# Hash attention and an MLP mixer on one core: three head pairs sorted by two hash bits where there were two

## The chip, the core and the metric

The kernel runs on one core of a Trainium2 chip. The metric is device time in microseconds (us), the median of three runs of one compiled program; profiles are of one further execution. TensorE is called PE in profile lines (its weight loads PEld), VectorE DVE, ScalarE ACT, GpSimd POOL, and SyncE SP; SP and POOL issue the DMAs.

## The reference

Four batches of eight heads, 768 tokens, head size 64. Each token of q and k gets a bucket from the signs of six projections, and a query attends only to keys of its own bucket. The heads side by side make a 768 x 512 matrix per batch, which goes through a mixer over tokens and one over channels. The weights come as 64-bit floats.

```python
q_bucket = np.sum((np.einsum('bhsd,dk->bhsk', q, proj) > 0) * powers, axis=-1)   # k_bucket likewise
mask = q_bucket[:, :, :, None] == k_bucket[:, :, None, :]
scores = np.where(mask, scale * np.matmul(q, k.transpose(0, 1, 3, 2)), -1000000000.0)
attn = np.exp(scores - np.max(scores, axis=-1, keepdims=True))
x = np.matmul(attn / (np.sum(attn, axis=-1, keepdims=True) + 1e-09), v)          # heads are then put side by side
u = x + (np.maximum(x.transpose(0, 2, 1) @ w_tok1, 0.0) @ w_tok2).transpose(0, 2, 1)
out = u + np.maximum(u @ w_ch1, 0.0) @ w_ch2
```

## The kernel before

**Stages.** The program has three stages: attention, tokens, channels. Attention works on 16 pairs of heads, numbered 0 to 15; pair n is heads 2(n mod 4) and the next of batch n // 4. `XT` holds the result, channels on partitions, and is the working copy of the activations to the end. A guard that is computed along the way chooses a slower exact path if scores could overflow; it isn't taken with these inputs. The order of instructions within a stage is the order of the code.

**A regular pair** (0 to 13). PE makes scores, `scores` (L487), the 6-bit mask added through a product of bits; ACT takes the exponential into `exps` (L414); DVE adds the exponentials over key blocks into `esd` (`add` and `add_last`, L446 to L459); PE sums `esd` with a product by ones (L536) and weighs v (`weigh`, L470); DVE makes reciprocals (`newton`, L549 and L551, ACT copying rows at L557) and multiplies (`divide`, L561). The loop over pairs (L1012) interleaves this: while pair n is scored, pair n-1 is divided. Hash bits of a pair two ahead are made in between and spread by DMAs of SP (L373) and POOL (L376).

**The conversion of weights.** A 768-column piece of 64-bit weights becomes 32-bit in one ACT instruction (L177) and five DVE instructions (L187, L191, L195, L196, L206). Attention converts twelve pieces, one in each of pairs 0, 1 and 3 to 12: first the token weights `W1` (two pieces) and `W2` (two), then eight of the channel weights `WC1`. Tokens converts eight pieces of the second channel weight.

**A sorted pair** (14 and 15, class `Sorted`). Two of the six bits put every token in one of four groups of 256 slots, so that scores are needed only within a group. Its steps are hung into the loop of the regular pairs by the dictionary `SORTED` and the calls of `at`, in three numbers `(first, made, back)`. In pair `first` the tokens are hashed and counted; in the next three, POOL writes 24 blocks of rows into tables in DRAM (`scatter`, L791, eight in each, alternating with the bit DMAs); in the pair ahead of `made`, SP fetches the sorted rows (L801 to L809) and DVE turns q (`turn_q`, L820); at `newton` of pair `made`, DVE turns k (L820) and the bits (`turn_sorted_bits`, L833). At the end of pair `made`, after the regular weighing, PE makes the sorted scores (L848), sums and weighing (L862, L874), and DVE divides and turns back (L889 to L899) ahead of the next pair's adds. SP writes the result in slot order (L902). POOL then gathers twelve blocks back to token order (`gather`, L908), in pairs `back` and the next, the last four each followed by two small memsets (`pause`, L940), and SP stores them (L918).

**Order between the stages.** Token matrices (tokens on partitions) pass through DRAM, one matrix `bounced` per batch: `bounce` transposes two pairs on DVE (L233) and SP writes them (L238). `fetch` (L245) reads a batch into `x0` (batches 0, 2) or `x1` (1, 3). SP runs its DMAs in order, so what waits at its head holds all behind it. `x0` of batch 0 is fetched at the end of pair 12. In pair 13 two more pairs are bounced (`bounce_late`), right after `newton`; then comes the fetch of `x1` for batch 1. Sorted pairs must also reach `XT`: SP reads them back (`fetch_turned`, L929) and DVE transposes them there (`finish`, L935) at the end of attention.

**Tokens** runs, per batch b, `mix1(b)` (24 passes of PE at L1222), then the second product of batch b-1 in two halves (`mix2`, L1262) with five DVE additions each (L1277 to L1281); POOL adds each half to `XT` by a DMA (L1282). `mix2` has three buffers, and its PSUM banks come free as DVE reads them. Channels (L1349 and around) follows, nearly all PE.

## Time and profile before

| | us |
|---|---|
| median of three runs (lowest, highest) | 768.08 (767.57, 768.83) |
| profiled execution, its own time | 766.84 |
| its span on the core | 765.1 |
| attention, to the first product of tokens | 288.05 |
| tokens, to the first product of channels | 78.5 |
| channels | 398.5 |

The profiled execution is 1.24 us below the median of the runs, and 1.7 us of it lie around the span. PE counts as busy for 99% of the span and DVE for 88%, but PE's ends are modelled, so a busy PE says only that it has work queued; the rate is read from how far apart equal pieces start. Rows of the timeline give start, duration, engine, line, operation, what is written and read, how many, and in brackets how long the engine was idle before and what released it.

### The profile page before, as it was taken

The page shows a single profiled execution, that of the slowest core. Times are in us where ns is not written, and L with a number is a line of the kernel's source. Part 1 is how long each engine was busy: PE and PEld are TensorE (multiplying, and loading weights), DVE is VectorE, ACT ScalarE, POOL GpSimd, SP SyncE. Part 2 cuts the span into 40 slices and gives each one's busy share as a digit, 9 for nine tenths or more (in the row PEclk, how much of TensorE's full clock was granted, in tenths as well). Part 3 has the DMA queues.
Part 4 walks back from the last instruction along what each step waited for, and adds up shares of the span by engine and source line. Part 5 has one row for each costly group of instructions (what it writes and reads, how often), then busy time and mean ns, then how long its engine had stood idle before and what let it go on. Part 6 is the DMA issues. An engine that isn't in the chain of part 4 may idle for free.

```text
span 765.1 us, 14575 instructions
## 1 busy us (share of the span) xinstructions
PE 757.4 (99%) x5549; PEld 507.8 (66%) x5549; DVE 672.7 (88%) x965; ACT 444.8 (58%) x820; POOL 188.5 (25%) x266
## 2 busy tenths in 40 slices
PE   8999999999999999999999999999999999999997
PEld 4555555665656554555444468888878888886886
DVE  5899899999998898999788798998899799889884
ACT  6677777677777773333222326566666667665331
POOL 2346772647761810011220100110000011000001
PEclk9999999999999999999999999999999999999999
DMA  7756578664965549876697997889566696750655
GB/s 257 271 172 178 179 243 231 199 207 142 222 198 117 168 67 263 313 168 123 113 316 253 349 359 259 246 227 280 169 220 212 236 259 141 233 158 10 205 162 126
DMA packets 131210, 157.80 MB, mean 206 GB/s; under 512 B 56000, under 2 KB 99520, under 8 KB 129216
## 3 DMA queue, kind: packets, MB, share of 16 engines
q1 hardware_dynamic: 119248, 136.05, 56.1%
q0 software_dynamic: 11600, 20.53, 13.2%
q8 instruction: 45, 0.74, 0.4%
q10 hardware_dynamic: 288, 0.25, 0.1%
q14 instruction: 29, 0.24, 0.1%
HBM read 107.71 MB, written 40.67 MB: 194 GB/s over the span
## 4 chain that ended last, share of the span: by engine, by line
PE 81%; DVE 12%; ACT 2%; issue 2%; DMA 1%; POOL 1%; DVEq 0%; ACTq 0%; SPq 0%; POOLq 0%
PE b L1349 51%; PE sc L503 12%; PE acc L470 11%; ACT exps L414 1%; PE sc L425 1%; DVE size L196 1%; DVE esd L459 1%; PE ss L848 1%; DVE unit L195 1%; PE hash L536 1%; PE sacc L874 1%; DMA XT<-second 1%; DVE second L206 1%; DVE size L191 1%; DVE unit L187 1%
## 5 line engine op out<-in xcount | busy, mean ns | idle before, releaser
L1349 PE MATMUL b<-R,second 128*128 128x256 f32 (+1 forms) x522 | 131.8, 408 | 0.0
L414 ACT ACTIVATE exps<-sc 128x768 f32<-128x768 f32 (+1 forms) x181 | 126.5, 765 | 8.9 <-PE sc L503 6.1
L503 PE MATMUL sc<-qk 32*128 32x384 f32 (+1 forms) x1352 | 119.3, 458 | 0.0
L1349 PEld LDWEIGHTS b<-R,second 128*128 128x128 f32 x522 | 99.2, 190 | 28.4 <-issue 16.5
L470 PE MATMUL acc<-exps,vn 128*32 128x385 f32 (+1 forms) x1344 | 111.7, 486 | 0.0
L503 PEld LDWEIGHTS sc<-qk 32*128 32x128 f32 x1352 | 91.7, 185 | 17.2 <-issue 4.5
L1355 ACT COPY c<-b 128x256 f32<-128x256 f32 (+1 forms) x96 | 40.3, 427 | 79.4 <-PE b L1349 66.1
L470 PEld LDWEIGHTS acc<-exps,vn 128*32 128x32 f32 x1344 | 43.8, 109 | 62.0 <-issue 59.6
L376 POOL DMA_DIRECT2D bits<-XT x104 | 54.5, 526 | 70.8 <-issue 38.6
L459 DVE TENSOR_TENSOR esd<-esd,exps 128x768 f32<-128x768 f32 x70 | 66.9, 956 | 4.3
L1349 PE MATMUL b<-XT,WC 128*128 128x256 f32 (+1 forms) x208 | 61.0, 428 | 0.0
L791 POOL DMA_INDIRECT table<-XT,sorting x48 | 56.3, 1173 | 15.0 <-issue 13.8
L2059 POOL DMA_DIRECT2D out<-second x7 | 8.5, 1213 | 186.8 <-DVE second L2053 81.7
L1349 PEld LDWEIGHTS b<-XT,WC 128*128 128x128 f32 x208 | 39.5, 190 | 15.4 <-issue 10.3
L503 PE MATMUL sc<-bits 32*128 32x384 bf16 (+1 forms) x338 | 48.0, 311 | 0.1
L557 ACT COPY rec<-rec 32x384 f32<-32x384 f32 x56 | 28.6, 510 | 33.0 <-DVE rec L551 31.5
L1349 PE MATMUL b<-XT,SW 128*128 128x256 f32 (+1 forms) x164 | 47.0, 410 | 0.0
L455 DVE TENSOR_TENSOR esd<-esd,exps 128x768 f32<-128x768 f32 x42 | 40.2, 958 | 4.4
L1222 PE MATMUL t<-x,W 128*128 128x512 f32 x96 | 42.1, 594 | 0.2 <-DMA x<-bounced 0.2
L1349 PEld LDWEIGHTS b<-XT,SW 128*128 128x128 f32 x164 | 31.1, 190 | 9.4 <-issue 4.1
L1282 POOL DMA_DIRECT2D XT<-second x8 | 9.9, 1233 | 97.6 <-DVE unit L187 58.0
L1222 PEld LDWEIGHTS t<-x,W 128*128 128x128 f32 x96 | 18.1, 190 | 23.3 <-issue 21.7
(332 smaller groups left out, 1452.7 us busy)
## 6 DMA issues: line engine op xcount, KB each, us to landing
second<-left SPq DMA_DIRECT2D x20, 768.0 KB
qk<-in_qk_rows SPq DMA_DIRECT2D x13, 1152.0 KB
raw<-in_moe_w_ch SPq DMA_DIRECT2D x16, 768.0 KB
second<-left SPq DMA_DIRECT2D x18, 576.0 KB
WC<-hidden_left SPq DMA_DIRECT2D x18, 448.0 KB
x<-bounced SPq DMA_DIRECT2D x4, 1536.0 KB
XT<-second POOLq DMA_DIRECT2D x8, 768.0 KB
seen<-in_qk SPq DMA_DIRECT2D x15, 384.0 KB
```

The lines of the kernel that those rows point to most:

```text
L376: nc.gpsimd.dma_start(out=to[at : at + 2 * BITS, half[j]], in_=g[of : of + 2 * BITS])
L414: return nc.scalar.activation(e[:, :, columns], sc, ACT.Exp, scale=SCALE)
L455: nc.vector.tensor_tensor(self.d, self.d, e, op=ALU.add)
L459: nc.vector.tensor_tensor(self.d, self.d, e, op=ALU.add)
L470: made = nc.tensor.matmul(acc[D * i + d : D * i + d + 32], vn[:, i, c, d : d + 32], e[:, i], start=(c == 0), stop=(c == NR - 1),)
L503: nc.tensor.matmul(made[j, piece][:, i], k[at : at + 32, ks], q[at : at + 32], start=part < 0, stop=part == 1,)
L557: nc.scalar.copy(rec[other : other + 32, h], rec[at : at + 32, h])
L791: nc.gpsimd.indirect_dma_start(out=tables[2 * w + i], out_offset=bass.IndirectOffsetOnAxis(ap=self.at[:, x : x + 1], axis=0), in_=row, in_ ...
L1222: nc.tensor.matmul(ps, W1[:, r, P * j : P * j + P], x[:, r], start=(r == 0), stop=(r == NR - 1),)
L1282: nc.gpsimd.dma_start(out=XT[:, 2 * m : 2 * m + 2, S * b : S * b + S], in_=to.rearrange("p i n t -> p i (n t)"), accum_op=ALU.add,)
L1349: nc.tensor.matmul(ps, left(k), right(k), start=start and k == ks[0], stop=stop and k == ks[-1], skip_group_check=True,)
L1355: nc.scalar.copy(c, ps)
```

## The change

`SORTED` gets a third entry, so pair 13 is sorted too and the loop has 13 regular pairs (0 to 12). Its third number is now how many scatters go in each of three pairs. The entries are 13: first 1, made 6; 14: first 4, made 9; 15: first 7, made 11. There are two sets of DRAM tables in place of one, the second cleared in pair 2. The channel weights are converted first, then `W1`, then `W2`, whose last piece falls in pair 12, now the last; until then `W1` and `W2` hold q, k and v of the sorted pairs.

For pair 15, `made` isn't `first + 5`, so its sorted rows are fetched at the end of pair 10, and all its turning stands at a new point, `turned`, in pair 11 behind the conversion. All 36 gathers stand behind POOL's last hash DMAs: ten in pair 11, ten in pair 12 and sixteen in tokens, each with a `pause`. The stores of pairs 14 and 15, `fetch_turned` (into `x0`, free after `mix1(2)`) and `finish` move into tokens, `finish` just ahead of the second product of batch 3. The bounce in the last pair comes after the first `divide`.

```diff
-    SORTED = {B * NP - 2: (1, 6, 9), B * NP - 1: (5, 10, 11)}
+    SORTED = {B * NP - 3: (1, 6, (8, 8, 8)), B * NP - 2: (4, 9, (8, 8, 8)), B * NP - 1: (7, 11, (10, 10, 4))}
...
+            for x, count in enumerate(counts):
+                at(first + 1 + x, "indirect", *[call("scatter")] * count)
+            if made == first + 5:
+                at(made - 1, "begin", call("fetch"))
+                at(made - 1, "last", call("turn_q"))
+                at(made, "sums", call("copy_bits"))
+                at(made, "newton", call("turn_k"), call("turn_sorted_bits"))
+            else:
+                at(made - 1, "last", call("fetch"))
+                at(made, "weighed", call("copy_bits"))
+                at(made, "turned", call("turn_q"), call("turn_k"), call("turn_sorted_bits"))
             at(made, "end", call("scores", 0), call("scores", 1), call("weigh"))
             at(made, "last", call("divide"), call("turn_back"))
...
+            gathers += [call("gather", r, i) for r in range(NR) for i in range(2)]
+            stores.append((n, call("store")))
+        for n in (NREG - 2, NREG - 1):
+            for _ in range(10):
+                at(n, "indirect", gathers.pop(0), pause)
+        for gather in gathers:
+            remaining.extend((gather, pause))
...
+        at(2, "loads", lambda: clear_tables(1))
+        at(NREG - 1, "newton", stores.pop(0)[1])
...
-            [(w_tok1, W1, 3, (0, NR)), (w_tok2, W2, 1, (0, NJ)), (w_ch1, WC1, 1, (0, NCB))],
+            [(w_ch1, WC1, 1, (0, NCB)), (w_tok1, W1, 3, (0, NR)), (w_tok2, W2, 1, (0, NJ))],
...
-            converts = n not in (2, NREG - 1)
+            converts = n != 2
...
             if n + 1 == NREG:
                 before.divide()
+                bounce(pool.tile([P, 2 * S], F32, name="stage", tag="stage", bufs=1), NREG - 3)
                 before = Quotients(halves)
...
             if converts:
                 weights.turnover()
+            now_at(n, "turned")
             halves[1].weigh(acc)
...
             fetch(1, x1)
             jobs = jobs(weights(pool))
-            bounce(places[2], NREG - 2)
+            bounce(places[2], NREG - 1, 1)
+            while remaining:
+                remaining.pop(0)()
...
-            if not turned and b + 2 < B:
-                fetch(b + 2, x)
+            if not turned and b == 0:
+                fetch(2, x)
+                stores[0][1]()
...
             mix1(b)
+            if b == 2 and not turned:
+                fetch_turned()
...
                 mix2(b - 1, 1)
+                if not turned and b == 1:
+                    stores[1][1]()
+                    fetch(3, x1)
+        finish()
         mix2(B - 1, 0)
```

Three places show how instructions moved. The first is DVE in the pair that makes the last sorted pair: pair 10 before. L549 and L551 are `newton`, L820 and L833 the turning of k and of the bits, L459 adds exponentials, L187 to L206 convert a piece of weights.

```order
L549 TENSOR_TENSOR rec_2910<-hash_2857,near_2873 128x384
L551 SCALAR_TENSOR_TENSOR rec_2910<-rec_2910,near_2873 128x384 x2
L820 STREAM_TRANSPOSE x0_110<-XT_81 128x8x2x32 x2
L833 STREAM_TRANSPOSE x0_110<-x0_110 128x512 x2
L459 TENSOR_TENSOR esd_2866<-esd_2866,exps_121 128x768 x3
L187 TENSOR_SCALAR unit_2955<-size_2925 128x768
L191 TENSOR_SCALAR size_2925<-size_2925 128x768
L195 SCALAR_TENSOR_TENSOR unit_2955<-raw_2722,unit_2955 128x768
L196 TENSOR_TENSOR size_2925<-size_2925,unit_2955 128x768
L561 TENSOR_TENSOR XT_81<-num_2711,rec_2910 128x768
L206 SCALAR_TENSOR_TENSOR WC1_85<-raw_2722,size_2925 128x768
```

And pair 11 of the changed kernel on DVE, where the same instructions have lines 3 to 18 higher (L838 turns q and k, L851 the bits):

```order
L552 TENSOR_TENSOR rec_3346<-hash_3298,near_3312 128x384
L554 SCALAR_TENSOR_TENSOR rec_3346<-rec_3346,near_3312 128x384 x2
L462 TENSOR_TENSOR esd_3305<-esd_3305,exps_122 128x768 x3
L187 TENSOR_SCALAR unit_3390<-size_3357 128x768
L191 TENSOR_SCALAR size_3357<-size_3357 128x768
L195 SCALAR_TENSOR_TENSOR unit_3390<-raw_3145,unit_3390 128x768
L196 TENSOR_TENSOR size_3357<-size_3357,unit_3390 128x768
L564 TENSOR_TENSOR XT_81<-num_3134,rec_3346 128x768
L206 SCALAR_TENSOR_TENSOR W2_109<-raw_3145,size_3357 128x768
L838 STREAM_TRANSPOSE x0_110<-XT_81 128x8x2x32 x4
L851 STREAM_TRANSPOSE x0_110<-x0_110 128x512 x2
```

The transposes stood behind `newton`; they now stand behind the adds, the conversion and the division, and are six where they were four.

The second place is DVE in the last pair, from its `newton` on, before (`raw` is the buffer that `bounce_late` transposes into):

```order
L459 TENSOR_TENSOR esd_3682<-esd_3682,exps_121 128x768 x3
L549 TENSOR_TENSOR rec_3696<-hash_3675,near_3689 128x384
L551 SCALAR_TENSOR_TENSOR rec_3696<-rec_3696,near_3689 128x384 x2
L233 STREAM_TRANSPOSE raw_3704<-XT_81 128x24x32 x2
L561 TENSOR_TENSOR XT_81<-num_3521,rec_3696 128x768
L549 TENSOR_TENSOR rec_3747<-hash_3675,near_3744 128x384
L551 SCALAR_TENSOR_TENSOR rec_3747<-rec_3747,near_3744 128x384 x2
L561 TENSOR_TENSOR XT_81<-num_3735,rec_3747 128x768
L935 STREAM_TRANSPOSE XT_81<-stage_3562 128x768 x2
L233 STREAM_TRANSPOSE second1_3792<-XT_81 128x24x32 x2
```

And of the changed kernel (DVE, last pair, from the same `newton`):

```order
L552 TENSOR_TENSOR rec_3703<-hash_3652,near_3666 128x384
L554 SCALAR_TENSOR_TENSOR rec_3703<-rec_3703,near_3666 128x384 x2
L187 TENSOR_SCALAR unit_3745<-size_3715 128x768
L191 TENSOR_SCALAR size_3715<-size_3715 128x768
L195 SCALAR_TENSOR_TENSOR unit_3745<-raw_3397,unit_3745 128x768
L196 TENSOR_TENSOR size_3715<-size_3715,unit_3745 128x768
L564 TENSOR_TENSOR XT_81<-num_3383,rec_3703 128x768
L233 STREAM_TRANSPOSE stage_3751<-XT_81 128x24x32 x2
L552 TENSOR_TENSOR rec_3765<-hash_3652,near_3762 128x384
L554 SCALAR_TENSOR_TENSOR rec_3765<-rec_3765,near_3762 128x384 x2
L206 SCALAR_TENSOR_TENSOR W2_109<-raw_3397,size_3715 128x768
L564 TENSOR_TENSOR XT_81<-num_3741,rec_3765 128x768
```

Four instructions of a conversion and a division now stand between `newton` and the transposes that the bounce waits for.

The third place is SP at the start of tokens, before, from the second bounce into batch 3 on:

```order
L238 DMA bounced3_91<-second1_3792 32x24x64 x4
L169 DMA raw_3843<-in_moe_w_ch2 128x3x512
L245 DMA x0_110<-bounced2_90 128x6x512
L169 DMA raw_3871<-in_moe_w_ch2 128x3x512
L169 DMA raw_3889<-in_moe_w_ch2 128x3x512
L245 DMA x1_3801<-bounced3_91 128x6x512
```

And SP of the changed kernel at the same point (L936 is `store`):

```order
L238 DMA bounced3_91<-second1_3809 32x24x32 x4
L169 DMA raw_3907<-in_moe_w_ch2 128x3x512
L245 DMA x0_110<-bounced2_90 128x6x512
L936 DMA bounced3_91<-XT_81 128x6x32 x4
L169 DMA raw_3939<-in_moe_w_ch2 128x3x512
L169 DMA raw_3957<-in_moe_w_ch2 128x3x512
L169 DMA raw_3993<-in_moe_w_ch2 128x3x512
L936 DMA bounced3_91<-XT_81 128x6x32 x4
L245 DMA x1_3818<-bounced3_91 128x6x512
```

The fetch of batch 3 now stands behind two stores, which wait for POOL's gathers, and behind one more fetch of weights.

More of the change, by code (lines that the diff above doesn't have):

```diff
@@ L378, in spread @@
                             between.pop(0)()
-                assert not between
+                for job in between:
+                    job()
         def first_hashes(half):
@@ L949, in now_at @@
                 job()
-        for n, (first, made, back) in SORTED.items():
+        gathers = []
+        for n, (first, made, counts) in SORTED.items():
             it = Sorted(n)
@@ L962, in attention @@
             at(first + 1, "begin", call("places"), call("numbers"), call("put_bits"))
-            for n in range(4 * NR):
-                at(first + 1 + n // 8, "indirect", call("scatter"))
-            at(made - 1, "begin", call("fetch"))
-            at(made - 1, "last", call("turn_q"))
-            at(made, "sums", call("copy_bits"))
-            at(made, "newton", call("turn_k"), call("turn_sorted_bits"))
+            for x, count in enumerate(counts):
+                at(first + 1 + x, "indirect", *[call("scatter")] * count)
@@ L970, in attention @@
             at(made, "last", call("divide"), call("turn_back"))
-            for r in range(NR):
-                for i in range(2):
-                    x = 2 * r + i
-                    if back + 1 == NREG - 2:
-                        at(back + x // 8, "indirect", call("gather", r, i))
-                        if x >= 8:
-                            at(back + 1, "indirect", pause)
-                    else:
-                        at(back + r // (NR // 2), "indirect", call("gather", r, i))
```

134 lines of the change are left out of this document (71 added, 63 removed).

## The prediction

> **What bounds the kernel now.** I read the page first, then the stretches of single pairs, then the timeline of the last pairs and of the start of tokens on every engine. From the page, the busy shares and the chain that ended last:
>
> ```profile
> PE 757.4 (99%) x5549; PEld 507.8 (66%) x5549; DVE 672.7 (88%) x965; ACT 444.8 (58%) x820; POOL 188.5 (25%) x266
> PE 81%; DVE 12%; ACT 2%; issue 2%; DMA 1%; POOL 1%; DVEq 0%; ACTq 0%; SPq 0%; POOLq 0%
> ```
>
> PE is the bound almost everywhere, DVE stands close behind. Three stretches from one pair's first product to the next one's (start and end, length, then busy us of PE, PEld, DVE, ACT, POOL): a plain pair, one that also hashes a sorted pair, one that also scores and weighs a sorted pair.
>
> ```profile
> 83.54:101.89 18.35, 18.35 (x250) 10.49 (x254) 16.40 (x22) 14.09 (x23) 14.19 (x17) 1.00 0.52 162
> 101.89:121.74 19.85, 19.85 (x270) 11.63 (x274) 19.06 (x27) 15.54 (x26) 12.77 (x19) 1.00 0.95 252
> 121.74:149.69 27.95, 27.95 (x410) 17.81 (x414) 26.46 (x46) 20.78 (x39) 10.43 (x15) 1.00 0.65 224
> ```
>
> A regular pair costs PE 18.35 us, a sorted one 1.50 + 9.60 = 11.10. DVE is busy 16.4 to 19.1 us in a pair, so whatever DVE must finish for PE at a pair's end comes late. That is the second fact, and the timeline of pairs 10 to 13 shows it:
>
> ```profile
> 219.13 1.29 DVE L820 STREAM_TRANSPOSE x<-XT 128x512 f32<-128x512 f32 x2
> 220.35 1.26 DVE L833 STREAM_TRANSPOSE x<-x 128x512 bf16<-128x512 bf16 x2
> 223.53 4.08 PE L848 MATMUL ss<-x 32*128 32x256 bf16 x80
> 229.17 1.85 DVE L233 STREAM_TRANSPOSE stage<-XT 128x768 f32<-128x768 f32 x2
> 233.13 0.34 PE L503 MATMUL sc<-bits 32*128 32x192 bf16 x4
> 237.32 0.92 DVE L450 SCALAR_TENSOR_TENSOR esd<-exps 128x768 f32<-128x768 f32 x1
> 251.79 0.34 PE L503 MATMUL sc<-bits 32*128 32x192 bf16 x4
> 253.61 0.95 DVE L206 SCALAR_TENSOR_TENSOR WC<-raw,size 128x768 uint32<-128x768 uint32 x1
> 254.70 0.96 DVE L450 SCALAR_TENSOR_TENSOR esd<-exps 128x768 f32<-128x768 f32 x1
> 263.22 0.56 DVE L549 TENSOR_TENSOR rec<-hash,near 128x384 f32<-128x384 f32 x1 [1.38 <-ACT near L541]
> 269.49 0.34 PE L503 MATMUL sc<-bits 32*128 32x192 bf16 x4
> 271.68 0.95 DVE L206 SCALAR_TENSOR_TENSOR WC<-raw,size 128x768 uint32<-128x768 uint32 x1
> 272.55 0.95 DVE L450 SCALAR_TENSOR_TENSOR esd<-exps 128x768 f32<-128x768 f32 x1
> ```
>
> Turning (L820, L833) ended at 221.61, 1.9 us ahead of the sorted scores (L848, 223.53). But the conversion of pair 11 (L206) ended at 254.56, 2.8 us after pair 12's first product at 251.79; that of pair 12 at 272.63, 3.1 us after pair 13's at 269.49.
>
> **The change part by part.** *PE's work.* A regular pair goes, a sorted one comes: -18.35 + 1.50 + 9.60 = -7.25 us, if nothing waits.
>
> *Turning for pair 14* (pair 9, behind `newton` as before). The 1.9 us of slack in pair 10 was without a bounce in the pair ahead; pair 8 bounces (1.85, L233), and the placing of pair 15's tokens is new there too. So 0 to 2, and I take +0.5, near nothing since the slack and the bounce are equal.
>
> *Turning for pair 15* (pair 11). It stands behind the conversion, and PE's sorted scores, and pair 12 behind them, wait for it. DVE's start there: 2.8 us late as in pair 12 of before, and pair 10's bounce of 1.85 on top: 4.6 us after the pair's first product. From the first add to the end of L206, pair 12 took 254.70 to 272.63, less 1.38 idle that a late start takes up: 16.55. Turning: twice 1.22 (219.13 to 220.35) and 1.26. Sum 4.6 + 16.55 + 2.44 + 1.26 = 24.9. PE is through its pair after 269.49 - 251.79 = 17.7. The wait is 7.2; with a semaphore's time, +7.3. From below: without the bounce's lag 5.4; with a late fetch of the sorted rows 9. Queued behind the waiting PE are all later products.
>
> *The last pair* follows a sorted one, so its adds start as in pair 11 of before, 237.32 - 233.13 = 4.2 after the pair's first product, where they started 272.55 - 269.49 = 3.1. Its sums wait for the adds already:
>
> ```profile
> 264.40 2.15 ACT L557 COPY rec<-rec 32x384 f32<-32x384 f32 x4 [1.22 <-DVE rec L551]
> 266.57 0.97 ACT L177 ACTIVATE size<-raw 128x768 f32<-128x768 f32 x1
> 267.73 0.55 DVE L187 TENSOR_SCALAR unit<-size 128x768 uint32<-128x768 uint32 x1
> 270.81 0.95 DVE L561 TENSOR_TENSOR XT<-num,rec 128x768 f32<-128x768 f32 x1
> 282.79 0.55 DVE L549 TENSOR_TENSOR rec<-hash,near 128x384 f32<-128x384 f32 x1
> 283.39 0.85 PE L536 MATMUL hash<-esd,ones 128*32 128x384 f32 x8
> 284.44 1.83 DVE L233 STREAM_TRANSPOSE raw<-XT 128x768 f32<-128x768 f32 x2
> 286.30 3.10 SPq L238 DMA_DIRECT2D bounced<-raw  x4
> 288.05 10.57 PE L1222 MATMUL t<-x,W 128*128 128x512 f32 x24
> 289.58 1.03 SPq L245 DMA_DIRECT2D x<-bounced  x1
> 289.58:298.85 9.27, 9.04 (x23) 3.67 (x21) 6.92 (x8) 2.90 (x6) 0.00 (x0) 1.00 0.93 283
> 298.85 10.57 PE L1222 MATMUL t<-x,W 128*128 128x512 f32 x24 [0.23 <-DMA x<-bounced]
> ```
>
> So +1.1. Tokens then start at 288.05 - 7.25 + 0.5 + 7.3 + 1.1 = 289.7.
>
> *The fetch of batch 1.* Before, it was issued at 289.58 and PE took it up at 298.85, after only 0.23 idle; DMA engines were 93% busy meanwhile. SP holds it behind the last bounce, and that behind DVE. Now a conversion stands ahead of the bounce. Count from T, the start of tokens: `newton` at T - 5.26 (282.79 to 288.05); from there ACT's copies and L177 let L187 start 267.73 - 263.22 = 4.51 later, at T - 0.75 (adds covered this in pair 12; here nothing does); to the end of the division 3.95 (267.73 to about 271.68), T + 3.2; transposes 1.83, T + 5.0; SP 3.3 (286.27 to 289.58), T + 8.35; landing 9.27, T + 17.6. PE wants it at T + 10.57: a wait of 7.05, 6.8 more than now. From below 0, if the fetch lands much faster. [...]
>
> *Gathers.* POOL's pace, and who follows it:
>
> ```profile
> 245.82 0.48 POOL L376 DMA_DIRECT2D bits<-XT  x1 [14.67 <-issue]
> 259.74 0.52 POOL L376 DMA_DIRECT2D bits<-XT  x1
> 267.58 1.07 POOL L908 DMA_INDIRECT XT<-result,sorting  x1 [0.21 <-issue]
> 268.65 0.99 POOL L940 MEMSET sorting<- 128x256 bf16 x2
> 269.82 0.96 POOL L908 DMA_INDIRECT XT<-result,sorting  x1 [0.18 <-issue]
> 270.94 2.41 SPq L918 DMA_DIRECT2D bounced<-XT  x4
> 337.85 10.46 PE L1222 MATMUL t<-x,W 128*128 128x512 f32 x24
> L908 POOL DMA_INDIRECT XT<-result,sorting x24: 960/1076/1563, 200.5 to 269.8; - x24
> L1282 POOL DMA_DIRECT2D XT<-second x8 | 9.9, 1233 | 97.6 <-DVE unit L187 58.0 <-DVE second L1281 16.6 <-ACT second L1270 6.3
> ```
>
> With a pause a gather takes 2.24 us (267.58 to 269.82). POOL reaches its first at pair 10's start (233.13 - 18.35 + 1.5 + 0.5 = 216.8) plus 12.7 (233.13 to 245.82) plus some 11 (bits and gathers took 13.9 to 259.74; four fewer here): 240.5. The 36th starts at 319, the store of pair 15 at 320 (1.12 later, as 269.82 to 270.94), issued by 323, landed by about 325 (no row; 0 to 3 us); then batch 3's fetch lands 9.27 later, 334, or some 340 if the weight fetches ahead of it wait for late conversions. PE wants it at 289.7 + 17.6 + 39.0 (298.85 to 337.85) = 346. Cost 0; the cover is 6 to 12 us, and it is thin only if PE is not late.
>
> *What else moves costs nothing.* `finish`, now three transposes of 0.92 at the end of tokens: DVE works on while PE waits 6.8 for batch 1, and gets more ahead than these 2.75; without that cover, 0 to 2.75. Its twelve reads are SP's last in tokens. Clearing the second tables writes 1.6 MB, 6 us at the 283 GB/s above, beside loads for pairs two and three ahead. The order of weights alone changes no length.
>
> Sum: -7.25 + 0.5 + 7.3 + 1.1 + 6.8 = +8.45. On the profiled execution's 766.84 that is 775.3; on the median of 768.08, which is 1.24 above it, **776.5 us**.
>
> **The rivals.** *One of the two long waits is missing* (22%): 8.45 - 7.3 = +1.15 or 8.45 - 6.8 = +1.65, so 769.2 or 769.7. For it: each rests on a lag of DVE worked out over a whole pair. Against: both follow from an order that can't change.
>
> *The saving stays with PE* (13%), faster: DVE is early enough in pair 11 and the fetch lands by T + 10.6. Then only 1.1 comes back, tokens start at 281.9, and batch 3 is wanted at 281.9 + 49.8 (288.05 to 337.85) = 331.7 against 334: -7.25 + 1.1 + 1.9 = about -4.2, 763.9. It decides at DVE: the turning would have to end 17.7 us into pair 11, not 24.9. DVE's 88% over the span speaks for room, its rows of pairs 11 and 12 against.
>
> *POOL is held off by DVE in tokens* (5%), slower still: gathers late, so batch 3 late. At the longest rows (1.56 for a gather, 0.99 for its memsets, 0.5 between) sixteen gathers take 3.05 in place of 2.24, 13 us in all: 334 becomes 347, +0.6, 777.1. The Trainium skill (SBUF — State Buffer, A bandwidth-pool intuition that's wrong) gives 3.1 us for a POOL DMA beside a DVE copy where it takes 0.62 alone; by an estimate from that, batch 3 lands near 367 and the time is about 797. Rows against it: POOL's DMAs in tokens (L1282) took 1.23 us, in attention (L908) 1.08.
>
> That the change doesn't do what it says is no case: the order shows 13 regular pairs.
>
> **How the numbers follow.** My forecast has 60%, rivals 22, 13 and 5. About 0.2%, or 1.5 us, is what a measurement of this kernel tells from no change. Slower by more: forecast, third rival and half of the first, 76%. Within: the other half, 11%. Faster: 13%. The range takes in the first rival (down to 769, and 768 with its own slack) and the upper ends of the forecast (turning 9, +1.7; pair 9's wait 2, +1.5; later stalls): 768 to 781. It leaves out the faster case and most of the third.
>
> **What would show it.** In the changed profile: an idle PE of 5 to 9 us ahead of the sorted scores in pair 11, released by DVE; tokens starting near 289.7, not 281; an idle PE of some 7 us ahead of batch 1's first product, released by the fetch; none ahead of batch 3's; channels 398 us as now. I am wrong if the first product of tokens starts before 284, or if batch 1 is taken up at once.

## The result and the profile after

The changed kernel took 795.36 us (median of four runs, 789.93 to 799.88) beside 768.25 for the kernel before on the same chip: a ratio of 1.0356, 95% interval 1.0326 to 1.0385. It is slower, as forecast, but by 27 us where 8.45 were worked out. Its runs lie 10 us apart; those of before 1.3. The profile is of the execution that took 795.21 us.

From the page of the changed kernel, the rows that answer to those of before, and the granted clock in the span's 40 slices:

```profile
PE 760.3 (96%) x5483; PEld 509.5 (64%) x5483; DVE 670.6 (85%) x975; ACT 439.0 (55%) x819; POOL 248.8 (31%) x361
PEclk9999999999999898898999999999999999999999
PE 87%; DMA 8%; DVE 2%; issue 1%; ACT 1%; SPq 1%; POOL 0%; DVEq 0%; ACTq 0%; POOLq 0%
```

PE is now idle for 33 us of a span of 793.5, DMAs stand in the chain, and four slices between 258 and 377 us have a lower clock, which the kernel before never had. PE's waits, from the view that adds them up by line (total, number, longest):

```profile
PE t L1224 <- DMA x<-bounced: 7.5, 1, 7.5
PE t L1265 <- ACT second L1270: 7.1, 2, 6.7
PE ss L866 <- DVE x L851: 6.7, 1, 6.7
PE hash L350 <- DMA qk<-in_qk_rows: 4.0, 2, 2.1
```

Line numbers moved: L1224 is `mix1`, L1265 `mix2`, L866 the sorted scores, L350 the hash. The stretches from pair 10 to channels (start and end, length, busy us of PE, PEld, DVE, ACT, POOL, then granted clock, DMA share, GB/s):

```profile
222.34:242.05 19.71, 19.68 (x248) 11.68 (x248) 17.50 (x24) 14.81 (x26) 10.03 (x12) 1.00 0.35 111
242.05:259.82 17.77, 17.77 (x238) 10.38 (x234) 17.06 (x21) 14.25 (x24) 14.74 (x26) 1.00 0.83 191
259.82:266.50 6.68, 0.00 (x2) 0.01 (x3) 6.58 (x10) 0.83 (x3) 5.74 (x12) 0.77 0.72 221
266.50:277.90 11.40, 11.40 (x160) 8.09 (x162) 0.24 (x1) 5.34 (x10) 9.61 (x18) 0.84 0.09 17
277.90:297.56 19.66, 18.93 (x243) 11.11 (x242) 15.52 (x20) 15.24 (x27) 16.68 (x26) 1.00 0.54 143
297.56:308.13 10.57, 10.57 (x28) 4.48 (x24) 8.18 (x11) 3.72 (x8) 9.07 (x16) 1.00 0.47 86
308.13:315.59 7.46, 0.00 (x0) 0.00 (x0) 6.38 (x5) 0.60 (x1) 6.52 (x12) 0.70 1.01 322
315.59:328.87 13.28, 13.28 (x24) 5.75 (x25) 11.40 (x18) 2.29 (x3) 4.65 (x9) 0.78 1.01 292
328.87:356.12 27.25, 26.86 (x75) 13.79 (x73) 25.04 (x40) 10.33 (x19) 2.62 (x2) 1.00 0.89 209
356.12:362.85 6.73, 0.00 (x2) 0.00 (x1) 2.99 (x7) 1.32 (x3) 1.20 (x1) 0.71 1.07 321
362.85:366.33 3.48, 3.48 (x7) 2.00 (x8) 3.38 (x5) 1.19 (x3) 0.00 (x0) 0.58 1.26 209
366.33:394.69 28.36, 28.36 (x82) 15.20 (x81) 21.20 (x36) 9.66 (x19) 3.63 (x3) 1.00 0.71 119
```

Each long idle stretch (6.68, 7.46, 6.73 us) is followed by work that takes longer than its like: the sorted part of pair 15 took 11.40 for 9.60, batch 1's products 13.28 for the 10.57 of batch 0, three pairs of `mix2` products 3.48. The clock explains it. Around pair 11's wait, in the same columns:

```profile
259.82:263.30 3.48, 0.00 (x0) 0.00 (x0) 3.44 (x5) 0.83 (x3) 3.01 (x6) 1.00 0.89 236
263.30:270.10 6.80, 3.60 (x40) 2.79 (x44) 3.14 (x6) 0.00 (x0) 5.93 (x12) 0.51 0.30 105
270.10:277.90 7.80, 7.80 (x124) 5.31 (x118) 0.24 (x1) 5.34 (x10) 6.41 (x12) 0.99 0.09 18
```

The clock stays at 1.00 for 3.48 us of idling, falls to half, and is back after PE has worked for 3.60. The Trainium skill (TensorE: Matmul & The Clock Gate, What's actually happening) states just this: half rate after an idle window of some 3.4 us, full rate after as long a busy one. The trace agrees at this wait; some shorter waits, at the end of this document, brought the slow clock too, and there the measurement decides. The prediction had no price for a slow clock.

Channels are unchanged: 793.5 - 394.69 = 398.8 us, 398.5 before. The loss between the two profiled executions is 297.56 - 288.05 = 9.5 us at the start of tokens and 97.13 - 78.53 = 18.6 in tokens. The third wait is the one that no step of the prediction held. SP and ACT around it, from the timeline (SP's durations reach from the first issue of a row to its last):

```profile
321.31 8.20 SPq L936 DMA_DIRECT2D bounced<-XT  x4
329.63 5.33 SPq L169 DMA_DIRECT2D raw<-in_moe_w_ch  x3
335.13 5.74 SPq L936 DMA_DIRECT2D bounced<-XT  x4
347.33 0.36 SPq L245 DMA_DIRECT2D x<-bounced  x1
347.80 2.05 SPq L169 DMA_DIRECT2D raw<-in_moe_w_ch  x2
```

```profile
361.53 0.89 ACT L177 ACTIVATE size<-raw 128x768 f32<-128x768 f32 x1 [8.77 <-DMA raw<-in_moe_w_ch]
362.32 0.47 ACT L1270 COPY second<-t 128x384 f32<-128x384 f32 x1
```

Pair 15's store (L936) goes out at 335.13; the fetch of batch 3 (L245) waits for its last bytes until 347.33; two weight fetches (L169) stand behind that. ACT takes its work in order too, so the size step of a weight conversion (L177) holds the copy (L1270) that PE needs. Batch 3 was in time; the weights behind it were not.

### The profile page after: what moved, and what is told of

It is laid out like the page before. It is cut to its first block, busy times and chain, and to the rows that moved or that the text cites. A ratio compares the mean times of both kernels' runs of the same rounds, so it can differ in the third digit from the quotient of the medians.

```text
span 793.5 us, 14576 instructions
## 1 busy us (share of the span) xinstructions
PE 760.3 (96%) x5483; PEld 509.5 (64%) x5483; DVE 670.6 (85%) x975; ACT 439.0 (55%) x819; POOL 248.8 (31%) x361
## 4 chain that ended last, share of the span: by engine, by line
PE 87%; DMA 8%; DVE 2%; issue 1%; ACT 1%; SPq 1%; POOL 0%; DVEq 0%; ACTq 0%; POOLq 0%
PE b L1374 50%; PE sc L506 12%; PE acc L473 11%; PE t L1224 3%; PE t L1265 3%; DMA qk<-in_qk_rows 2%; PE ss L866 2%; DMA raw<-in_moe_w_ch 2%; PE sc L428 1%; PE sacc L892 1%; DMA x<-bounced 1%; DMA bounced<-XT 1%; DMA XT<-table 1%; PE hash L539 1%; PE ssums L880 1%
## 5 line engine op out<-in xcount | busy, mean ns | idle before, releaser
L417 ACT ACTIVATE exps<-sc 128x768 f32<-128x768 f32 (+1 forms) x168 | 117.2, 773 | 10.9 <-PE sc L506 7.0
L506 PE MATMUL sc<-qk 32*128 32x384 f32 (+1 forms) x1248 | 112.5, 458 | 0.0
L473 PE MATMUL acc<-exps,vn 128*32 128x385 f32 (+1 forms) x1248 | 103.9, 486 | 0.0
L506 PEld LDWEIGHTS sc<-qk 32*128 32x128 f32 x1248 | 85.8, 185 | 14.3 <-issue 3.3
L811 POOL DMA_INDIRECT table<-XT,few x72 | 84.9, 1179 | 22.1 <-issue 19.1
L473 PEld LDWEIGHTS acc<-exps,vn 128*32 128x32 f32 x1248 | 40.6, 109 | 57.4 <-issue 55.6
L378 POOL DMA_DIRECT2D bits<-XT x96 | 50.7, 530 | 54.3 <-DVE XT L368 27.4
L462 DVE TENSOR_TENSOR esd<-esd,exps 128x768 f32<-128x768 f32 x65 | 62.2, 956 | 4.0
L1224 PE MATMUL t<-x,W 128*128 128x512 f32 x96 | 44.9, 627 | 7.5 <-DMA x<-bounced 7.5
L506 PE MATMUL sc<-bits 32*128 32x384 bf16 (+1 forms) x312 | 44.7, 311 | 0.1
L926 POOL DMA_INDIRECT XT<-result,few x36 | 40.1, 1115 | 9.3 <-issue 6.8
L458 DVE TENSOR_TENSOR esd<-esd,exps 128x768 f32<-128x768 f32 x39 | 37.4, 958 | 4.8 <-ACT exps L417 0.9
L1224 PEld LDWEIGHTS t<-x,W 128*128 128x128 f32 x96 | 19.2, 202 | 32.3 <-issue 23.2
```

Source lines behind the costliest of these rows:

```text
L378: nc.gpsimd.dma_start(out=to[at : at + 2 * BITS, half[j]], in_=g[of : of + 2 * BITS])
L417: return nc.scalar.activation(e[:, :, columns], sc, ACT.Exp, scale=SCALE)
L458: nc.vector.tensor_tensor(self.d, self.d, e, op=ALU.add)
L462: nc.vector.tensor_tensor(self.d, self.d, e, op=ALU.add)
L473: made = nc.tensor.matmul(acc[D * i + d : D * i + d + 32], vn[:, i, c, d : d + 32], e[:, i], start=(c == 0), stop=(c == NR - 1),)
L506: nc.tensor.matmul(made[j, piece][:, i], k[at : at + 32, ks], q[at : at + 32], start=part < 0, stop=part == 1,)
```

## The experiments

**Theory.** Each wait is an order in a queue (DVE in pair 11, SP at batch 1, SP and then ACT in `mix2`), and the slow clock follows each idle stretch. **Rivals.** The DMA engines are too full, with three pairs' 128-byte rows, for any order to help; or DVE is the bound and gives back what it puts off. Ratios are to the kernel before on the same chip; the change alone has 1.0356. By its time, no other single edit than the turning and the bounce can be told from the change, whose interval is 1.0326 to 1.0385; what the others show is read from their waits. A profile is of one execution, and its time can lie some us off the median (791.13 for 786.42 in the run of the bounce). Line numbers shift by a few between these kernels.

**Turning ahead of the conversion in pair 11**, its fetch ahead of the bounce.

```diff
-                at(made - 1, "last", call("fetch"))
+                at(made - 1, "end", call("fetch"))
...
             now_at(n, "weighed")
+            now_at(n, "turned")
...
-            now_at(n, "turned")
             halves[1].weigh(acc)
```

> Edit: in pair 11 the turning of the sorted rows stands ahead of the weight conversion and the division on DVE, and the fetch of these rows stands ahead of the bounce on SP in pair 10. Theory (DVE's order sets the wait): turning ends some 3.7 us after 258.1, PE's wait falls from 6.68 to about 2, the sorted scores go from 5.89 back to 4.1 to 5, and what DVE puts off fits into its 11 us of idle time beside the sorted products: 5 to 6.5 us less at the start of tokens, 789 to 790.5 in all unless later waits take it. Rival (DVE is the bound and gives back later what it put off): tokens start within 1.5 us of 297.6, and the time is 794 or more.

Measured 788.12 us, ratio 1.0255 (1.0187 to 1.0324). The sorted scores in its PE timeline:

```profile
260.68 4.08 PE L866 MATMUL ss<-x 32*128 32x256 bf16 x80 [1.76 <-DVE x L851]
```

The wait falls to 1.76, the scores are back at 4.08, and tokens start at 290.01: 7.55 us earlier, of which the wait and its clock are 6.7. DVE gives nothing back there. But tokens then take 98.2 us.

**Bounce of pairs 10 and 11 behind batch 1's fetch.**

```diff
-                bounce(pool.tile([P, 2 * S], F32, name="stage", tag="stage", bufs=1), NREG - 3)
...
             fetch(1, x1)
             jobs = jobs(weights(pool))
+            bounce(places[1], NREG - 3)
```

> Edit: the bounce of pairs 10 and 11 moves from the last pair of attention to tokens, behind the fetch of batch 1 in SP's order. Theory (the fetch waits only for its place in SP's order): it is issued some 1.5 us after tokens start instead of 8.2, PE's wait of 7.46 us ahead of batch 1 shrinks below 1, and the products of batch 1 take 10.6 us again instead of 13.44, if a clock that falls after an idle stretch is what slowed them: 10 us less at the start of mix2. The later wait in mix2 of batch 1 (6.73) may grow by as much as PE comes earlier, since the stores ahead of it keep their time: so 785.5 to 792. Rival (the fetch is slow because gathers and other transfers run beside it): 4 us or more of the wait are left, and the time is above 791 for that reason.

Measured 786.42 us, ratio 1.0230 (1.0202 to 1.0258). PE in tokens:

```profile
297.13 20.87 PE L1224 MATMUL t<-x,W 128*128 128x512 f32 x48
321.78 0.91 PE L1265 MATMUL t<-W2sums,r 128*128 128x384 f32 x2 [2.49 <-DVE r L1249]
330.19 0.91 PE L1265 MATMUL t<-W2sums,TA 128*128 128x384 f32 x2 [2.34 <-ACT second L1270]
332.98 11.41 PE L1224 MATMUL t<-x,W 128*128 128x512 f32 x24
358.36 1.65 PE L1265 MATMUL t<-W2sums,r1s 128*128 128x384 f32 x2 [6.88 <-ACT second L1270]
```

Batches 0 and 1 run through in 20.87 us, without a wait and at full clock. Of the 10 us expected, two new waits in `mix2` of batch 0 take 4.8, and the old one stays: tokens take 93.5.

**Filling batch 1's wait** with eight products that nobody reads.

```diff
+            if b == 1 and not turned:
+                ps = bank("t1")
+                for i in range(8):
+                    right = W1[:, i % 3 * 2 : i % 3 * 2 + 2].rearrange("p r d -> p (r d)")
+                    nc.tensor.matmul(ps, W1[:, i % NR, :P], right, start=i == 0, stop=i == 7)
```

> Edit: ahead of batch 1's products, where PE stood idle for 7.46 us, it computes eight further products (128x512, some 7 us at the 0.44 us of a half) that nobody reads; nothing is left out. Theory (the clock falls because PE is idle): the granted clock stays at 1.00 there, batch 1's 24 products take 10.6 us again instead of 13.44, and mix2 starts 2.9 us earlier; of that the later wait in mix2 of batch 1 takes back up to 2.9, since the weights it waits for keep their time: 792.5 to 795. Rival (the clock falls because DMA, DVE and POOL are busy at that time, or PE's products are slowed by the transfers): the 24 products take 13 us or more as before.

Measured 791.84 us, ratio 1.0325 (1.0304 to 1.0347). The filled stretch and batch 1's products:

```profile
302.50:309.67 7.17, 6.85 (x17) 2.71 (x16) 5.57 (x4) 0.60 (x1) 6.44 (x10) 1.00 0.99 327
309.67:320.10 10.43, 10.43 (x25) 4.69 (x26) 9.19 (x14) 2.32 (x3) 5.54 (x10) 1.00 0.98 282
```

With DMA about as full as in the changed kernel (0.98 against 1.01), the clock is 1.00 and the products take 10.43 instead of 13.28. Idling brought the slow clock, not the transfers beside it. The time saved went to waits in `mix2` (3.06 us in batch 0, 5.18 in batch 1): tokens take 97.8.

**The waits in pairs 6 and 9** (1.97 and 2.05 us for queries and keys): first the fetch of sorted rows behind the load of queries and keys, then the row loads of the next sorted pair behind the fetch.

```diff
-                at(made - 1, "begin", call("fetch"))
+                at(made - 1, "added", call("fetch"))
```

> Edit: in pairs 5 and 8 the fetch of the sorted rows stands behind the load of a later pair's queries and keys on SP, not ahead of it. Theory (the row loads of the next sorted pair, which are new ahead of that fetch, make the queries and keys late): the two waits of PE for them, 1.97 and 2.05 us in pairs 6 and 9, go, and tokens start 4 us earlier: 791.4, unless later waits take it. Rival (the DMA engines are full there, 81 and 82 per cent busy, and whatever stands second is late): the sorted rows come late instead, and PE waits 2 us or more ahead of the sorted scores of these pairs; the time stays within 1.5 us of 795.4.

```diff
-            at(first, "last", call("load_rows"))
+            rows_at = (first, "last") if first == 1 else (first + 1, "added")
+            at(*rows_at, call("load_rows"))
...
-            at(first + 1, "begin", call("places"), call("numbers"), call("put_bits"))
+            at(first + 1, "begin", call("places"), call("numbers"))
+            at(first + 1, "begin" if first == 1 else "added", call("put_bits"))
```

> Edit: in pairs 5 and 8 the row loads of the next sorted pair stand behind the fetch of the sorted rows on SP, as for the kernel before, and no longer ahead of it; the places of the bits in these rows move with them. Theory (the row loads ahead delay the fetch, and the queries and keys behind it): PE's waits of 1.97 and 2.05 us in pairs 6 and 9 go, and none comes ahead of the sorted scores instead, as it did when the fetch was moved behind the queries and keys: 4 us less at the start of tokens, 791 if later waits don't take it. Rival (the scatters, which then start later, run late): a wait of 2 us or more for sorted rows in pair 9 or 11.

Measured 792.41 us, 1.0291 (1.0242 to 1.0340), and 794.45 us, 1.0373 (1.0322 to 1.0423). Both remove the waits for queries and keys, and in each another comes. From the first, PE; from the second, DVE and PE:

```profile
209.52 5.77 PE L866 MATMUL ss<-x 32*128 32x256 bf16 x80 [2.40 <-DVE x L851]
```

```profile
220.20 0.96 DVE L564 TENSOR_TENSOR XT<-num,rec 128x768 f32<-128x768 f32 x1 [7.67 <-DMA table<-XT,few]
```

```profile
223.38 0.34 PE L506 MATMUL sc<-bits 32*128 32x192 bf16 x2 [5.02 <-DVE unit L907]
```

Rows fetched later make the sorted scores late; rows loaded later are scattered later, and DVE's division must write where they lie. So row loads ahead of the fetch look like a price of packing three pairs. These waits are unsteady: in the other kernels, with this order untouched, they were 0 to 3.45 us.

**Who makes the weights late in `mix2`?** Four edits. Pair 15's store by POOL:

```diff
-            stores.append((n, call("store")))
+            stores.append((n, call("store") if n + 1 < B * NP else call("store", nc.gpsimd)))
...
                 remaining.pop(0)()
+            stores[1][1]()
...
                 if not turned and b == 1:
-                    stores[1][1]()
                     fetch(3, x1)
```

> Edit: the four stores of pair 15 are issued by POOL behind its last gather, and no longer by SP ahead of batch 3's fetch and two weight fetches. Theory (SP's order holds the weights): SP issues those weight fetches at some 340 us of the span instead of 347.8, ACT's size step (L177) and the copies of mix2 (L1270) behind it are on time, and PE's wait of 6.73 us in mix2 of batch 1 goes, with the slow clock behind it (three pairs of products took 3.48 us for 1.93): 8.2 us less, 787.2. Rival (the transfers themselves are slow, since one weight fetch took 13.65 us beside batch 3's fetch): the wait stays at 5 us or more, and the time within 2 us of 795.4.

The weights by POOL:

```diff
+            if bufs == 3:
+                self.queue = nc.gpsimd
...
-            nc.sync.dma_start(out=raw.rearrange("p (t n) w -> p t (n w)", t=rows), in_=src)
+            self.queue.dma_start(out=raw.rearrange("p (t n) w -> p t (n w)", t=rows), in_=src)
```

> Edit: in tokens all weight fetches but the first two are issued by POOL, which has issued its last gather at 320 us, and no longer by SP behind the stores and batch fetches. Theory (SP's order makes the weights late, and ACT waits for them ahead of its copies): PE's wait in mix2 of batch 1 (6.73 us) falls below 1 and its slow clock with it; 8 us less, 787. The run with the stores on POOL left 3.49 of that wait, because POOL issued the four stores 5 us apart and batch 3's fetch stayed ahead of the weights on SP. Rival (the store and the fetch of batch 3 take the bandwidth): a weight fetch still takes over 10 us, ACT still waits 5 us or more, and the time stays above 792.

No reads of turned rows, so that the results of the sorted pairs are missing from the sum:

```diff
-            if b == 2 and not turned:
-                fetch_turned()
```

> The changed kernel without the twelve reads of the three sorted pairs and their transposes at the end of tokens (those pairs' results are left out of the sum); they are 128-byte rows, and SP issues them from 350 us on, right behind the two weight fetches of which one took 13.65 us to land. Theory of load: that weight fetch lands in 9 us or less and PE's wait of 6.73 us falls by 4 or more: 790. Theory of order: the weights are issued at 347.8 as before, behind pair 15's store and batch 3's fetch; the wait stays at 5 us or more: 793 to 796.

And the weight conversion taken from ahead of the copies:

```diff
                 mix2(b - 1, 0)
-                job()
+                if b == B - 1:
+                    job()
```

> Edit: in tokens the weight conversions that stand between the two halves of mix2 of batches 0 and 1 go, and all later ones move down by one place, so that ACT's size step (L177), which waits for a weight fetch, no longer stands ahead of the copies (L1270) that PE waits for; nothing is left out, the conversions end 2 places later. Theory (order: PE waits 6.73 us only because ACT waits for a late weight in front of its copies): that wait falls below 1 with its slow clock, batch 3's fetch still lands in time: 787 to 789. Rival (batch 3's fetch, issued at 347.3 and landing 9 to 14 us later, is now wanted at 359 and is itself late): 2 us or more of wait ahead of batch 3's first product, 790 or more.

| edit | us | ratio (interval) | PE's wait in `mix2` of batch 1 | tokens, us |
|---|---|---|---|---|
| store by POOL | 792.00 | 1.0318 (1.0300 to 1.0336) | 3.49 | 93.7 |
| weights by POOL | 796.15 | 1.0358 (1.0305 to 1.0411) | 5.52 and 3.52 | 101.7 |
| no turned reads | 795.83 | 1.0385 (1.0332 to 1.0438) | 6.84 | 96.8 |
| weights later | 794.26 | 1.0368 (1.0333 to 1.0403) | none | 95.5 |

The 128-byte reads aren't it: without them the wait is as long. SP's order is part of it, since with the store off SP the wait halves, but not all: the weights come late from POOL too, where a fetch issued at 340 us, beside batch 3's, was there at 355. So the transfers are slow there as well, as the first rival has it; how much of the wait is their load was not separated. What passes it on to PE is that ACT waits for the weights ahead of the copies: with the conversion one place later PE's wait is gone. The kernel's time hardly moves (1.0368 against 1.0356). PE at batch 3 and at the start of channels in that last run, and SP:

```profile
353.52 10.46 PE L1224 MATMUL t<-x,W 128*128 128x512 f32 x24
390.93 5.92 PE L1375 MATMUL b<-XT,WC 128*128 128x512 f32 x8 [7.22 <-DVE second L1283]
```

```profile
345.53 18.92 SPq L1298 DMA_DIRECT2D x<-bounced  x12
364.56 2.05 SPq L169 DMA_DIRECT2D raw<-in_moe_w_ch  x1
```

Batch 3 starts 12.8 us earlier than in the changed kernel (2.1 of them from an earlier start of tokens), and at once; then 7.22 us come back ahead of channels, behind DVE, at a slow clock. The edit has its own part in them: the last weight fetch now stands behind the turned reads on SP and goes out at 364.56, its conversion ends at 377.7, and from there DVE works without a gap up to the additions that channels wait for. How little DVE has to spare is read from tokens as a whole, before and after:

```profile
288.05:366.58 78.53, 78.20 (x213) 39.37 (x210) 73.05 (x112) 28.71 (x53) 7.46 (x6) 1.00 0.79 211
```

```profile
297.56:394.69 97.13, 82.55 (x213) 41.22 (x210) 78.57 (x117) 29.09 (x55) 27.70 (x41) 0.91 0.84 197
```

DVE was busy for 73.05 of 78.53 us before; now it has 78.57 to do there: the rest of the last pair behind its conversion, a third transposed pair, the bounces. Its slack of 5.5 us is spent. That every us in which it waits for weights is then a us of tokens is argued from these sums; no run shows it by itself.

**Together.** Turning and bounce; the same with weights by POOL and row loads behind; the same two with weights later; and that without the turned reads.

> The two edits that took a wait away when they stood alone: bounce of pairs 10 and 11 behind the fetch of batch 1, and turning ahead of the conversion in pair 11. Theory (two waits, each with its own slow clock): tokens start near 290 and batch 1 is taken up at once; the wait in mix2 of batch 1 stays near 7 us, and that in mix2 of batch 0 (2.5 and 2.3 us, as in the run with the bounce moved) too: 779 to 784. Rival (what comes earlier to tokens only waits longer there for the weights and stores): the time stays at 786 or more, as with one of the two edits.

> All four: bounce of pairs 10 and 11 behind the fetch of batch 1, turning ahead of the conversion in pair 11 with its fetch ahead of the bounce, the weights of tokens fetched by POOL, and the row loads behind the fetch of sorted rows. Theory (each wait is an order in a queue, and with the slow clock behind it they are the whole loss): what is left is the 7.25 us saved, less 1.8 of waiting in pair 11, 1.1 in the last pair and some 3 of small delays, so 766 to 769, level with the kernel before or slightly under it. Rival (a third sorted pair loads the DMA engines and queues so that some wait comes back elsewhere): 775 or more.

> The same with the bounce of pairs 10 and 11 behind the fetch of batch 1 and the turning ahead of the conversion in pair 11 (784.5 with these two alone, where PE waited 4.65 and 4.96 us in mix2 of batches 0 and 1). Theory (order): both of these waits fall below 1, with some 2 us of slow clock behind them: 772 to 775. Rival (the fetch of batch 2 or 3 is the next in line, and comes 5 us or more after PE wants it): 778 or more.

> The run with the weights one place later, the bounce behind batch 1's fetch and the turning ahead of the conversion (783.4), without the twelve reads of the sorted pairs' results and their transposes in tokens (these results are left out of the sum). In that run SP issued the reads from 335.6 to 358.4 us and only then the last weight fetch, ACT waited for it until 366.5, PE 7.84 us in mix2 of batch 2, and 4.86 us ahead of channels. Theory (order, and the reads are the last of it): both waits go with their slow clock; tokens take 79 to 82 us instead of 95.5 (78.5 before the change), and the time is 768 to 772. Rival (the DMA engines as a whole bound tokens, whatever stands where: 95.5 us of tokens in both runs with the weights later, 97 before): tokens still take 88 us or more, 778 or more.

| edits | us | ratio (interval) | first product of tokens | tokens, us |
|---|---|---|---|---|
| turning, bounce | 784.48 | 1.0190 (1.0139 to 1.0240) | 288.44 | 95.3 |
| and weights by POOL, row loads behind | 790.72 | 1.0320 (1.0295 to 1.0344) | 291.28 | 97.6 |
| turning, bounce, weights later | 783.36 | 1.0219 (1.0202 to 1.0237) | 290.70 | 95.5 |
| and no turned reads | 780.62 | 1.0178 (1.0143 to 1.0213) | 289.49 | 88.3 |

The start of tokens is won each time; tokens get clearly shorter only in the last, which leaves work out. In the third, SP issued the reads ahead of the last weight fetch (335.57, 22.79 us), and PE waited 7.84 us for it in `mix2` of batch 2; in the fourth this wait is gone. What the reads cost is less clear: the third's profile is of an execution of 789.97 us, 6.6 above its median, and by the medians they cost 2.7 us, with intervals that overlap. The 4.86 ahead of channels stay, against what was expected: without the reads 4.89 us are left. PE and the end of DVE's last conversion in the fourth, and that conversion before:

```profile
377.74 6.13 PE L1373 MATMUL b<-XT,WC 128*128 128x512 f32 x8 [4.89 <-DVE second L1283]
366.14 0.96 DVE L206 SCALAR_TENSOR_TENSOR second<-raw,size 128x768 uint32<-128x768 uint32 x1
```

```profile
351.66 0.96 DVE L206 SCALAR_TENSOR_TENSOR second<-raw,size 128x768 uint32<-128x768 uint32 x1
```

So the theory of orders holds for the waits behind SP and ACT, and its sum does not: tokens need 88.3 us, not 79 to 82. The rival of DMA engines that are too full had named 88 or more, but PE's waits that are left are not for DMAs: these 4.89 and 2.36 in `mix2` of batch 0 are behind DVE, 0.92 in two pieces behind ACT and DVE, and ACT waited for weights only 2.0 us in all of tokens; without PE's waits it would be 80. The 4.89 are in part an order again: putting the weights later also brings the last conversion to within 10.6 us of channels, where it was 14.0 before, and DVE works through it and the last additions without a gap from 360.5 to 377.7. There the rival, DVE as the bound, has its part; that is argued from DVE's busy time, since no run took work from DVE alone. No version beat the kernel before: turning and bounce take back about half of the loss, and for the rest the runs show where it lies, not a way to take it away.

**Stores ahead, gathers without pauses.** The first form (811.38 us alone, 799.97 with turning and bounce) put pair 14's store ahead of four of its gathers, so it stores rows that aren't there yet; gathers waited 40.91 us for it and PE 21.5 us for weights behind. In a right order, with 24 gathers in pairs 11 and 12, and turning and bounce as above:

```diff
-            for _ in range(10):
-                at(n, "indirect", gathers.pop(0), pause)
+            for _ in range(12):
+                at(n, "indirect", gathers.pop(0))
...
             jobs = jobs(weights(pool))
+            stores[0][1]()
...
                 fetch(2, x)
-                stores[0][1]()
+                stores[1][1]()
+            if not turned and b == 1:
+                fetch(3, x1)
```

> The same, with the bounce of pairs 10 and 11 behind the fetch of batch 1 and the turning ahead of the conversion in pair 11 (784.5 with these two alone). Theory of order: the waits in mix2 of batches 0 and 1 that were left there (2.46, 4.65 and 4.96 us) fall under 2 each: 774 to 778. Rival, load: the sum of the waits for weights in tokens stays at 8 us or more, and the time at 782 or more.

> Edit: the 36 gathers of the changed kernel without the two fills of zeros on POOL behind each; all else in its place. In the two runs with all gathers in attention and no pauses, from 284 to 302 us PE was busy 3.9 of 6 us and less, DVE and ACT nearly idle, POOL issuing gathers; whether the lack of pauses did that or the stores beside them is open. Theory (gathers back to back hold back what the other engines are to execute): pair 12 takes 25 us or more in place of 19.7, until its ten gathers are through, and tokens start at 303 or later. Rival (the stores of 128-byte rows did it, or a tie of gathers to PE's products): pair 12 takes within 1 us of 19.7, and the time is 794 to 797, as with pauses.

Measured 805.58 us, 1.0481 (1.0461 to 1.0501) and 790.77 us, 1.0333 (1.0305 to 1.0360) for the pauses alone. In the first, the wait in `mix2` of batch 1 is gone (6.5 us behind ACT are left in that of batch 0) and tokens take 88.0 us, but pair 12 takes 40.7 instead of 19.7:

```profile
284.00:302.00 18.00, 9.88 (x23) 3.48 (x22) 2.85 (x3) 1.62 (x2) 12.16 (x13) 0.58 0.55 136
302.00:318.00 16.00, 15.76 (x150) 8.37 (x151) 9.97 (x13) 10.77 (x18) 0.00 (x0) 0.83 0.00 1
```

For 18 us DVE and ACT hardly work while POOL gathers. The theory that missing pauses do this falls: without them alone, and with ten gathers in the pair instead of twelve, pair 12 runs its 19.7 us. The right order without turning and bounce showed the same stall, with times from 798.22 to 814.58 us where 787 to 789 were expected. What caused the stall stays open.

## Why the prediction was right in sign and wrong in size

Between the profiled executions the loss was 28.1 us: the forecast 8.45, another 7.9 by the start of tokens and another 11.8 in tokens. The two long waits came as worked out. What failed is the cost of 0 for the gathers and the stores behind them, 7.1 us of waits, and that no step had a term for a slow clock, which took 1.8 + 2.7 + 1.55 = 6.1 us. The loads of queries and keys, 4.0 us, come third.

*PE's work, -7.25, and the last pair, +1.1*: right; the last pair took 19.66 for 18.56, and with the terms below the sum closes to 3.2 us.

*Pair 9, +0.5*: the turning there cost nothing. Instead PE waited 1.97 and 2.05 us in pairs 6 and 9 for queries and keys. I had followed the turning, not the other loads on SP that the new row loads move.

*Pair 11, +7.3*: right in mechanism and size, 6.68. DVE's rows:

```profile
258.05 0.55 DVE L187 TENSOR_SCALAR unit<-size 128x768 uint32<-128x768 uint32 x1
...
262.77 2.48 DVE L838 STREAM_TRANSPOSE x<-XT 128x512 f32<-128x512 f32 x4
265.18 1.26 DVE L851 STREAM_TRANSPOSE x<-x 128x512 bf16<-128x512 bf16 x2
```

Turning ended at 266.44, 24.4 us into the pair (24.9 forecast), and the edit shows that its place did it. Missing was the clock behind it: 1.8.

*Start of tokens, 289.7*: measured 297.56, +9.5 for +1.65. Waits and clock above are 1.97 + 2.05 + 1.8 of the difference; less 0.6 in pair 11 and 0.5 in pair 9; another 3.2 are spread over pairs that show no wait, as pair 10, 19.71 for the 18.66 (233.13 to 251.79) of the pair behind a sorted one before. Not all of it belongs to the change: in five further runs with the same attention, tokens started at 291.91 to 297.13.

*Batch 1, +6.8*: right. Issue at T + 8.17 (8.35 forecast), landing 9.82 later (9.27), wait 7.46, 7.23 more than before. The clock added 2.7, as the filled wait shows.

*Gathers, "Cost 0"*: the step that failed. The 36th was issued at 318.96 (319 forecast), by luck: the first came at 246.2, not 240.5, and they followed each other every 2.08 us, not 2.24. Batch 3 was not late. But the store that was to go at 320 went at 335.13, behind pair 14's store (8.20 us on SP) and weight fetches (5.33), and landed at 347.18, not 325; and I asked only for batch 3, which PE wants late, not for the weights queued behind it, which ACT wants early. Cost: 6.73, 0.39 in batch 0, and 1.55 of slow clock (3.48 for the 1.93 of three pairs of products that elsewhere start 0.64 apart). This is what PE lost there; the edit that took the wait away did not shorten the kernel, since the late weights then held PE ahead of channels.

*`finish` covered*: DVE "gets more ahead", I wrote. Its 5.5 us of slack in tokens were used up; that this is why moving one wait brought another is argued, not shown.

Tokens add up: 7.23 + 2.71 + 0.39 + 6.73 + 1.55 = 18.6.

*The second rival* has a slip in its sum: 334 - 331.7 is 2.3, not 1.9, so 764.2; nothing hangs on it.

*The third rival* came near in time (797 by the page on SBUF) and not in mechanism. POOL was not held off, with DVE beside it:

```profile
L926 POOL DMA_INDIRECT XT<-result,few x36 | 40.1, 1115 | 9.3 <-issue 6.8 <-PE sc L506 1.2 <-DMA XT<-table 1.0
```

A gather took 1.12 us, not the 3.1 that the Trainium skill (SBUF — State Buffer, A bandwidth-pool intuition that's wrong) gives for a POOL DMA beside a DVE copy; DVE ran no copy beside these gathers.

Open: how much of tokens is DVE's load alone, how much the load of the DMA engines, and what stopped the engines for 18 us.

## What to carry to other kernels

When a change moves DMAs, list for each queue everything behind the moved one, and for each of these the engine that waits for it in order and what stands behind that wait. Price a long wait of PE with the slow clock behind it (1.6 to 2.7 us here). Before counting on a wait being hidden, add up the moved engine's work in that stage: at 93% busy (73.05 of 78.53) there is little to hide it in.

## What was unexpected in the hardware

Short idle stretches can already bring the slow clock: 2.40 us of waiting ahead of pair 14's sorted scores did (below), 2.36 us in `mix2` of batch 0 in the last run of the second table did too (granted clock 0.57 from 314 to 318 us). But 2.05 us in pair 9 of the changed kernel did not, nor 2.41 in another run, nor 2.49 at the same place of `mix2` in the run of the bounce (1.00 from 321.78 to 327). So no length of wait, among these, divides the two.

```profile
207.10:209.52 2.42, 0.02 (x4) 0.01 (x2) 2.42 (x5) 1.52 (x3) 1.84 (x3) 1.00 0.89 328
209.52:213.90 4.38, 4.38 (x56) 3.58 (x60) 4.28 (x6) 2.53 (x6) 3.85 (x4) 0.61 1.06 239
```

Here the clock falls only when PE is already at work again. POOL's stores of 128-byte rows, issued one by one, went out 5 to 7 us apart, where SP issued four in 5.7 and in 8.2.
